# Attention pooling with a gated feed-forward layer on one core: the same instructions in another written-out order

## The chip, the cores and the metric

The kernel runs on one core of one Trainium2 chip. The metric is the device time of one execution in microseconds. The core has five engines, each with an instruction stream of its own that it works through in order: TensorE (PE, matmuls; its weight loads are listed as PEld), VectorE (DVE), ScalarE (ACT), GpSimd (POOL) and SyncE (SP). In this kernel the input loads are issued by POOL and the stores, and the copies inside the chip, by SP.

## The reference

Four batches of x (12480 rows of 128) meet 32 inducing rows I twice, and the result goes through one feed-forward layer:

```python
def mab(q, kv):
    s = scale * (q @ kv.transpose(0, 2, 1))
    s = s - s.max(-1, keepdims=True)
    a = np.exp(s)
    a /= a.sum(-1, keepdims=True) + 1e-09
    return a @ kv
h = mab(I, x)          # 32 rows for each batch: pooling over all of x
y = mab(x, h)          # every row of x attends to those 32 rows
u = y @ w_in           # 128 -> 2048
out = (u * np.clip(u + 3.0, 0.0, 6.0) / 6.0) @ w_out
```

## The kernel before, in words

Each batch is cut into six groups of 2048 rows and a short one (group 6) of 192 rows. For every batch there are two passes over the groups. The first is the pooling; it needs all groups of the batch before its result is there. Then a few small steps turn the 32 pooled rows into tables of the feed-forward layer. The second pass makes the output of every group out of its transposed rows, which are kept on the chip from the first.

The whole order of the work is one text, `ORDER` (lines 23 to 165): a list of tokens, each a call of a function `op_...` with its arguments: the batch, the group, a range or a part, the PSUM bank (0 to 7), and a letter for the engine where more than one can do it (V for DVE, A for ACT, P for POOL). The loop at lines 816 to 818 emits them one after the other, so the text fixes the order on every engine's queue. Tiles stand in small rings of buffers, and an instruction waits for those that it depends on.

First pass, for batch b and group g:
- `X` (line 416) loads rows of x into one of five xr buffers, issued on POOL's queue. A buffer is free when the casts and the last `A` of the group five before have read it.
- `K` (line 420) casts to bf16 on one of three engines, `T` (line 426) transposes 8 blocks of 128 rows on PE, `Y` (line 432) copies them out of PSUM.
- `S` (line 437) makes the scores with I on PE, `E` (line 445) the exponential on ACT, `A` (line 453) the weighted sums on PE, `H` (lines 464 and 466) adds them up on DVE, `D` (lines 471 and 473) adds up the weights.

Between the passes, for a batch: `c1` to `c9`, `cA` and `cB` (lines 477 to 526) with `c3` (lines 492 and 493), the sum of the weights over the partitions by two matmuls with ones; `G`, `L` and `cH` to `cN` (lines 545 to 589); 16 `M` (line 532, PE) with 16 `N` (line 540, Square on ACT); 16 `P` (line 598, PE) and `cP` (line 608).

Second pass, for a group:
- `Z` (line 621, PE) with `Zd` (line 631) and `Ze` (line 636), two exponentials on ACT. `Zd` writes one of two dk buffers.
- `W` (line 642): four copies by DMA from SP's queue, which spread dk over the partitions into one of two d buffers.
- `R` (line 650, PE), `Rl` (line 655, Ln on ACT), `Rz` (line 660, DVE), `Ra` (line 674, Exp on ACT), `Rh` (line 685, DVE).
- `B` (line 693, PE), `F` (line 703, Exp on ACT), `U` (line 712, DVE, which reads d), for the two halves of a group.
- `l` (line 729), `q` (line 747), both PE, add up the output in a bank; `v` (line 758) copies it out on DVE or ACT, and `O` (line 767) stores a group from SP's queue.

Four more tokens matter here. `it` (line 334) asks ACT for one activation table that has both Exp and Ln. ACT needs the right table for its functions, and where the order gives it another function than the table at hand has, the build puts a table load ahead of the instruction. `i1` (masks.py) makes the identity matrix on POOL, `i6` and `i7` constants there. `w.n.k` (line 353) is n matmuls of 512 columns over a tile of zeros into bank k, whose result nobody reads:

```python
def op_it(e):
    nc.scalar.preload_act_table_set("natural_log_exp_and_others")

def op_w(n, k):
    for _ in range(n):
        nc.tensor.matmul(ps[:, k, :], lhsT=wake[:, :P], rhs=wake)
```

The weights are loaded once (`wi`, `wo`, lines 393 and 396) and split or cast by `wh`, `wl` and `wb` (lines 403 to 409). At the end a few checks on ranges (`y0` to `yb`) give one flag; only if it is set does a slow path run (line 824).

Of the kernel before, what the change touches and what calls it, by code (L numbers as in the profile page):

```python
# [28 lines left out]
E.0.1.0.16.5 Y.0.2.8.16.3.A A.0.1.0.8.5 S.0.2.0.8.7 T.0.3.8.16.4 K.0.3.0.8.V S.0.2.8.16.7 D.0.1.V i6.P Y.0.3.8.16.4.V
i7.P A.0.1.8.16.5 E.0.2.0.16.7 T.0.3.0.8.2 H.0.0.1 wh.0.V H.0.1.5 wh.1.A A.0.2.0.8.7 Y.0.3.0.8.2.A wh.3.A wh.2.A  # L30
X.0.5.0.16 wl.1.V A.0.2.8.16.7 D.0.2.V K.0.4.0.8.V X.1.0.0.16 wo.- wl.2.V S.0.3.0.8.2 S.0.3.8.16.2 H.0.2.7 T.0.4.0.8.6
E.0.3.0.16.2 A.0.3.0.8.2 Y.0.4.0.8.6.A X.1.1.0.16 K.0.4.8.16.P K.0.5.8.16.P T.0.4.8.16.1 A.0.3.8.16.2 X.1.2.0.16
S.0.4.0.8.4 K.0.5.0.8.A D.0.3.V Y.0.4.8.16.1.V S.0.4.8.16.4 E.0.4.0.16.4 K.1.0.0.8.P T.0.5.0.8.5 wl.3.V T.0.5.8.16.1
Y.0.5.8.16.1.A Y.0.5.0.8.5.V A.0.4.0.8.3 S.0.5.0.8.5 A.0.4.8.16.3 S.0.5.8.16.5 H.0.3.2 E.0.5.0.16.5 K.1.0.8.16.V H.0.4.3
T.1.0.8.16.1 Y.1.0.8.16.1.A wb.1.A A.0.5.0.8.4 wb.0.A A.0.5.8.16.4 D.0.4.V D.0.5.V c1.0.- X.1.3.0.16 T.1.0.0.8.3 H.0.5.4
H.0.6.0 X.1.4.0.16 Y.1.0.0.8.3.A c3.0.6 K.1.1.0.8.P c5.0.7 c4.0.6 S.1.0.0.8.3 S.1.0.8.16.3 c6.0.7 c9.0.V wb.2.A
Z.0.1.2.7 c7.0.A Z.0.0.5.6 c8.0.V K.1.1.8.16.V wb.3.A G.0.1.4 E.1.0.0.16.3 Zd.0.1.2 T.1.1.0.8.3 T.1.1.8.16.0 cA.0.V
cB.0.V Ze.0.0.6 M.0.0.2 R.0.0.1 Zd.0.0.5 wl.0.V M.0.7.5 Ze.0.1.7 G.0.2.4 G.0.0.4 Y.1.1.8.16.0.V G.0.3.4 Rl.0.0.1
N.0.0.2.A Y.1.1.0.8.3.V M.0.2.1 M.0.3.0 M.0.6.2 K.1.2.8.16.P Rz.0.0.6 R.0.1.3 N.0.7.5.A M.0.1.6 N.0.2.1.A Rl.0.1.3
Rh.0.0.V cH.0.4 S.1.1.0.8.5 A.1.0.0.8.1 Rz.0.1.7 N.0.6.2.A S.1.1.8.16.5 M.0.8.3 A.1.0.8.16.1 M.0.10.7 M.0.5.2 N.0.3.0.A  # L40
W.0.0 P.0.2.0 K.1.2.0.8.P P.0.3.0 K.1.3.0.8.V H.1.0.1 E.1.1.0.16.5 T.1.2.8.16.1 M.0.9.5 D.1.0.V Rh.0.1.V N.0.1.6.A
N.0.10.7.A cJ.0.4 N.0.8.3.A T.1.2.0.8.7 T.1.3.0.8.3 M.0.4.6 Y.1.2.8.16.1.V M.0.11.1 K.1.3.8.16.P cI.0.4 P.0.1.0
X.1.5.0.16 Y.1.3.0.8.3.V N.0.9.5.A M.0.14.5 M.0.13.4 X.1.6.0.2 Ra.0.1 D.1.1.V K.1.4.8.16.P N.0.5.2.A Y.1.2.0.8.7.V
P.0.0.0 A.1.1.0.8.2 M.0.12.3 P.0.7.0 N.0.11.1.A N.0.13.4.A P.0.5.0 P.0.11.0 S.1.2.0.8.7 K.1.4.0.8.V P.0.9.0 A.1.1.8.16.2
Ra.0.0 H.1.1.2 N.0.4.6.A S.1.2.8.16.7 N.0.14.5.A N.0.12.3.A L.0.0.6 B.0.0.0.2.4 X.2.0.0.16 E.1.2.0.16.7 P.0.4.0
T.1.3.8.16.7 K.1.5.0.8.V L.0.1.6 F.0.0.0.1.4 P.0.14.0 Y.1.3.8.16.7.V W.0.1 Z.0.2.1.4 K.1.5.8.16.V Z.0.3.7.5 K.1.6.0.2.A
cL.0.6 F.0.0.0.0.2 M.0.15.3 P.0.12.0 P.0.6.0 Zd.0.3.7 Zd.0.2.1 cM.0.2 P.0.10.0 U.0.0.0 P.0.8.0 cN.0.2 N.0.15.3.A
T.1.6.0.2.1 Ze.0.2.4 P.0.13.0 P.0.15.0 B.0.0.1.2.6 Y.1.6.0.2.1.A T.1.5.0.8.1 cP.0.0 Y.1.5.0.8.1.V q.0.0.0.0.0
q.0.0.0.1.0 Ze.0.3.5 T.1.4.0.8.1 F.0.0.1.0.2 R.0.2.2 F.0.0.1.1.6 D.1.2.P Rl.0.2.2 U.0.0.1 Rz.0.2.4 K.2.0.0.8.V l.0.0.1.3
l.0.0.0.0 l.0.0.2.6 l.0.0.3.7 q.0.0.1.0.3 v.0.0.0.0.A Rh.0.2.V q.0.0.1.1.3 S.1.3.0.8.0 T.1.4.8.16.2 Y.1.4.0.8.1.A  # L50
v.0.0.1.3.A S.1.3.8.16.0 q.0.0.2.0.6 E.1.3.0.16.0 Y.1.4.8.16.2.V W.0.2 q.0.0.2.1.6 B.0.1.0.0.2 q.0.0.3.0.7 D.1.3.P
A.1.2.0.8.4 q.0.0.3.1.7 Ra.0.2 A.1.2.8.16.4 F.0.1.0.0.0 K.2.0.8.16.V v.0.0.2.6.V A.1.3.0.8.6 F.0.1.0.1.2 H.1.2.4 U.0.1.0
v.0.0.3.7.A B.0.2.0.0.2 T.1.5.8.16.7 F.0.2.0.1.2 F.0.2.0.0.0 A.1.3.8.16.6 l.0.1.0.4 Y.1.5.8.16.7.V q.0.1.0.0.4
q.0.1.1.0.7 B.0.2.1.2.0 H.1.3.6 S.1.4.0.8.6 q.0.1.0.1.4 v.0.1.0.4.V S.1.4.8.16.6 q.0.1.1.1.7 F.0.2.1.1.0 l.0.1.1.7
F.0.2.1.0.2 R.0.3.1 O.0.0.0.16 l.0.2.1.4 X.2.1.0.16 v.0.1.1.7.V E.1.4.0.16.6 l.0.2.0.0 U.0.2.0 Rl.0.3.1 q.0.2.1.0.4
B.0.1.1.6.2 Rz.0.3.5 A.1.4.0.8.1 q.0.2.0.0.0 F.0.1.1.1.2 F.0.1.1.0.6 D.1.4.V q.0.2.0.1.0 U.0.1.1 q.0.2.1.1.4 S.1.5.0.8.2
A.1.4.8.16.1 X.2.2.0.16 q.0.1.2.0.5 v.0.2.1.4.A S.1.5.8.16.2 q.0.1.3.0.7 Rh.0.3.V K.2.1.8.16.P Z.0.4.4.6 v.0.2.0.0.A
H.1.4.1 E.1.5.0.16.2 B.0.3.0.2.0 W.0.3 D.1.5.V Zd.0.4.4 q.0.1.2.1.5 q.0.1.3.1.7 A.1.5.0.8.4 K.2.1.0.8.P F.0.3.0.0.2
# [10 lines left out]
D.2.0.P q.0.4.0.0.3 M.1.0.5 l.0.4.0.3 Rh.0.6.V v.0.4.1.4.V F.0.4.1.0.6 F.0.4.1.1.0 N.1.0.5.A O.0.3.0.16 U.0.4.1
B.0.5.0.6.0 q.0.4.2.0.4 q.0.4.0.1.3 M.1.1.5 L.1.1.2 F.0.5.0.0.6 v.0.4.0.3.V cL.1.2 F.0.5.0.1.0 q.0.4.2.1.4 B.0.5.1.6.0  # L70
W.0.6 U.0.5.0 q.0.4.3.0.2 M.1.4.3 N.1.1.5.A F.0.5.1.1.0 l.0.4.2.4 N.1.4.3.A l.0.4.3.2 v.0.4.2.4.V M.1.8.5 F.0.5.1.0.6
q.0.5.0.0.0 q.0.4.3.1.2 N.1.8.5.A Z.1.0.3.1 Z.1.1.6.4 v.0.4.3.2.V Ra.0.6 Zd.1.0.3 S.2.1.0.8.2 M.1.10.5 l.0.5.0.0
q.0.5.0.1.0 S.2.1.8.16.2 M.1.5.3 Ze.1.0.1 P.1.2.7 Zd.1.1.6 U.0.5.1 v.0.5.0.0.V cM.1.6 R.1.0.0 O.0.4.0.16 P.1.3.7
# [906 lines left out]
```

## Time and profile before

| what | value |
|---|---|
| median of three runs | 308.41 us (304.93 to 309.09) |
| the profiled execution, its time | 310.61 us |
| its span, first to last instruction | 308.8 us |
| busy: PE, ACT, DVE, POOL | 275.8, 255.7, 218.5, 65.7 us |
| moved by DMA | 66.69 MB, mean 216 GB/s |
| shares of the chain that ended last | PE 64%, ACT 13%, DVE 9%, DMA 7%, issue 3% |

The busy time of PE counts each matmul from start to its modelled end, so overlapping ones hide how much room is left; how fast PE goes when nothing holds it is read from the chain of waits, where each piece is the time by which it moved the end. Prices of one instruction on the other engines are read from the groups by line.

### The profile page before, as it was taken

The numbers are of one execution on the slowest core, as the hardware profiler recorded it, in microseconds if no ns is written. First come the engines' busy times: TensorE is split into PE (matmuls) and PEld (weight loads), VectorE is DVE, ScalarE is ACT, GpSimd is POOL, SyncE is SP. The second block draws the span as 40 slices with busy tenths as digits, with TensorE's granted clock in tenths as the row PEclk, the third lists the DMA queues.
The fourth block names the chain that finished last, engine by engine and source line by source line (L and its number), as shares of the span: only waits on it lengthen the run. The fifth ranks groups of instructions, "written<-read, shape, count | busy, mean of one in ns | idle before, by whom it ended". The sixth has DMA issues, their size and how long they took to land.

```text
span 308.8 us, 9738 instructions
## 1 busy us (share of the span) xinstructions
PE 275.8 (89%) x4105; PEld 216.8 (70%) x4105; DVE 218.5 (71%) x386; ACT 255.7 (83%) x416; POOL 65.7 (21%) x101
## 2 busy tenths in 40 slices
...
GB/s 154 419 348 409 346 248 153 138 70 330 212 326 293 2 142 179 184 231 182 338 385 240 138 183 42 197 156 240 180 104 270 248 141 69 222 231 244 326 163 155
DMA packets 23312, 66.69 MB, mean 216 GB/s; under 512 B 3648, under 2 KB 16736, under 8 KB 16992
## 3 DMA queue, kind: packets, MB, share of 16 engines
...
q8 instruction: 33, 0.54, 0.7%
q14 instruction: 15, 0.12, 0.1%
...
## 4 chain that ended last, share of the span: by engine, by line
PE 64%; ACT 13%; DVE 9%; DMA 7%; issue 3%; SPq 1%; POOL 0%; ACTq 0%; DVEq 0%; POOLq 0%
PE ps L747 25%; PE ps L729 7%; PE ps L426 6%; PE ps L453 5%; DMA d<-dk 5%; PE ps L693 5%; PE ps L598 4%; PE ps L532 3%; ACT TF L703 3%; PE ps L621 3%; DMA xl<-in_x_dram 2%; PE ps L437 2%; ACT L655 2%; PE ps L650 2%; DVE TD L712 2%
## 5 line engine op out<-in xcount | busy, mean ns | idle before, releaser
L703 ACT ACTIVATE TF<-ps 128x1024 bf16<-128x1024 f32 (+1 forms) x100 | 96.2, 1005 | 8.8 <-PE ps L693 7.3
L712 DVE TENSOR_TENSOR TD<-TF,d 128x2048 bf16<-128x2048 bf16 (+1 forms) x52 | 61.1, 1177 | 13.3 <-ACT TF L703 11.7
L747 PE MATMUL ps<-Cq,TD 128*128 128x128 bf16 (+1 forms) x784 | 59.9, 222 | 0.1
L747 PE MATMUL ps<-Cq,TF 128*128 128x128 bf16 (+1 forms) x784 | 59.3, 221 | 0.2
L758 DVE COPY os<-ps 128x512 f32<-128x512 f32 x62 | 42.2, 688 | 22.8 <-PE ps L747 17.8
L747 PEld LDWEIGHTS <-TF 128*128 128x128 bf16 (+1 forms) x784 | 46.6, 99 | 11.2 <-issue 9.1
L747 PEld LDWEIGHTS <-TD 128*128 128x128 bf16 (+1 forms) x784 | 47.4, 100 | 6.9 <-issue 4.6
L729 PE MATMUL ps<-BD,a 128*128 128x512 f32 (+1 forms) x100 | 39.2, 463 | 0.0
L420 POOL CAST xb<-xr 128x1024 bf16<-128x1024 f32 x24 | 28.1, 1180 | 51.7 <-PE ps L426 39.1
L540 ACT ACTIVATE sq<-ps 128x512 bf16<-128x512 f32 x64 | 35.2, 617 | 1.5 <-PE ps L532 1.4
L453 PE MATMUL ps<-xr,a 128*32 128x128 f32 x384 | 31.8, 229 | 3.1 <-ACT ln L655 2.2
L426 PE MATMUL ps<-ident_b,xb 128*128 128x128 bf16 x384 | 30.8, 232 | 3.0 <-DVE xb L420 1.8
L432 DVE COPY xT<-ps 128x1024 bf16<-128x1024 bf16 x32 | 21.8, 687 | 13.0 <-PE ps L426 11.9
L453 PEld LDWEIGHTS ps<-xr,a 128*32 128x32 f32 x384 | 25.4, 111 | 5.6 <-ACT ln L655 3.0
L426 PEld LDWEIGHTS <-xb 128*128 128x128 bf16 x384 | 24.9, 105 | 6.1 <-issue 3.7
L693 PE MATMUL ps<-z,pair 32*128 32x256 f16 (+1 forms) x400 | 21.3, 272 | 7.9 <-ACT os L758 2.4
L416 POOL DMA_DIRECT2D xr<-in_x_dram x25 | 15.7, 630 | 49.5 <-PE ps L453 26.2
L532 PE MATMUL ps<-dH,w_hi 128*128 128x512 bf16 x64 | 22.2, 384 | 3.3 <-ACT dk L631 1.8
L758 ACT COPY os<-ps 128x512 f32<-128x512 f32 x34 | 19.7, 590 | 4.9 <-PE ps L747 2.7
L660 DVE CUSTOM_DVE_ANT_0 zz<-ln,ps 128x512 f32<-128x512 f32 (+1 forms) x28 | 17.3, 619 | 9.0 <-ACT ln L655 8.8
L729 PEld LDWEIGHTS ps<-BD,a 128*128 128x128 f32 (+1 forms) x100 | 18.3, 196 | 4.9 <-ACT dk L631 2.0
L432 ACT COPY xT<-ps 128x1024 bf16<-128x1024 bf16 x16 | 16.2, 1015 | 5.1 <-PE ps L426 5.1
...
## 6 DMA issues: line engine op xcount, KB each, us to landing
...
```

Of the source, the lines that this page charges most:

```text
L420: copier(e)(at(xb, xbl, b, g)[:p, lo:hi, :], at(xr, xl, b, g)[:p, lo:hi, :].bitcast(FP32))
L426: nc.tensor.transpose(pt[:, (i - lo) * p : (i - lo + 1) * p], at(xb, xbl, b, g)[:p, i, :], ident_b[:p, :p])
L432: copier(e)(xT_of(b, g)[:, lo * p : hi * p], ps[:, k, :].bitcast(BF16)[:, : (hi - lo) * p])
L453: nc.tensor.matmul(ps[:M, k, :C], lhsT=at(a1, a1l, b, g)[:p, i * M : (i + 1) * M], rhs=at(xr, xl, b, g)[:p, i, :], start=(i == 0), stop=(i ...
L532: nc.tensor.matmul(ps[:, k, :], lhsT=w_hi[:, jb, :], rhs=dH[:, :, :, :, :].rearrange("p q k m i -> p (q k m i)"),)
L540: nc.scalar.activation(sq_of(b, jb)[:, :], ps[:, k, :], ACT.Square)
L693: nc.tensor.matmul(ps[:, pairs[j // 2] + j % 2, f * w : (f + 1) * w], lhsT=pair[rows, f].rearrange("p m i -> p (m i)"), rhs=fat(z_, b, g)[ ...
L703: nc.scalar.activation(hat(TF_, b, g, h)[:, 2 * q : 2 * q + 2, :w], ps[:, k : k + 2, :w], ACT.Exp, scale=-1.0)
L712: nc.vector.tensor_mul(split(hat(TD_, b, g, h)), split(hat(TF_, b, g, h)), d.unsqueeze(2).to_broadcast([P, J, 2, w]),)
L729: nc.tensor.matmul(ps[:p, k, : J * C], lhsT=fat(a_, b, g)[:rows, s * p : (s + 1) * p], rhs=BD_[b % 2][:rows, :J, :].rearrange("p j c -> p ...
L747: nc.tensor.matmul(ps[:p, k, j * C : (j + 1) * C], lhsT=t[:, j, f * w + s2 * p : f * w + (s2 + 1) * p], rhs=Cq_[b % 2][:, (1 + f) if u els ...
L758: copier(e)(at(os_, osl, b, g)[:p, s * J : (s + 1) * J, :], ps[:p, k, : J * C].rearrange("p (j c) -> p j c", c=C),)
```

## The change

Only the text of `ORDER` is replaced: 1599 tokens in place of 1583, where the 16 more are all `w` (24 with 48 matmuls in place of 8 with 16, all of them in the pooling of batch 0). Every other operation is there as often as before. What differs is the place of each, the bank, and for some the engine:

| operation | before | after |
|---|---|---|
| K, cast of x | 26 P, 22 V, 4 A | 24 P, 17 V, 11 A |
| Y, copy of the transposed rows | 33 V, 19 A | 41 V, 11 A |
| v, copy of the output | 65 V, 35 A | 61 V, 39 A |
| D, sum of the weights | 15 V, 9 P | 12 V, 12 P |
| wh, wb, parts of the weights | 1 V 3 A, 4 A | 2 V 2 A, 2 A 2 P |

`it` is the first token; before, it stood in the middle of batch 1's tables. The first five loads of x stand ahead of everything else on POOL's queue, and the short group 6 of batch 0, which was first through PE, comes among the full ones. The diff, cut to the start and to the places that the text below speaks of:

```diff
-i0.- X.0.0.8.16 i1.- X.0.0.0.8 i2.- w.2.6 X.0.6.0.2 w.2.0 i4.5 K.0.6.0.2.A w.2.3 w.2.0 w.2.2 i3.V T.0.6.0.2.4 i8.- w.2.3
-w.2.7 i5.5.V X.0.1.0.16 i9.P X.0.2.0.16 ia.- K.0.0.8.16.V Y.0.6.0.2.4.A X.0.3.0.16 S.0.6.0.2.0 E.0.6.0.2.0 w.2.2
...
-v.0.2.3.2.V q.0.2.2.0.3 O.0.1.0.16 q.0.2.2.1.3 B.0.3.1.0.4 X.2.4.0.16 Y.2.0.0.8.7.A W.0.4 c3.1.7 K.2.2.0.8.P
...
-T.2.1.8.16.1 cA.1.V M.1.2.0 Zd.0.6.4 Ze.0.6.5 Rz.0.4.6 l.0.3.0.4 R.0.5.6 c9.1.P E.2.0.0.16.2 Y.2.1.8.16.1.A T.2.1.0.8.2
...
-N.1.10.5.A E.2.1.0.16.2 q.0.5.1.0.5 N.1.5.3.A Rl.1.0.0 M.1.11.3 M.1.7.2 D.2.1.P it.- N.1.7.2.A A.2.0.0.8.0 cN.1.6
...
+it.- i2.- X.0.0.0.8 w.2.2 X.0.0.8.16 X.0.1.0.16 w.2.5 X.0.2.0.16 w.2.3 w.2.1 X.0.3.0.16 i1.- w.2.2 i9.P w.2.6 w.2.7
+w.2.3 i0.- i3.V w.2.5 i4.3 w.2.7 K.0.0.0.8.A w.2.4 i8.- K.0.0.8.16.A w.2.6 T.0.0.0.8.2 X.0.6.0.2 ia.- T.0.0.8.16.0
+i5.3.V w.2.3 w.2.1 Y.0.0.8.16.0.A i6.P Y.0.0.0.8.2.V w.2.2 K.0.1.0.8.V K.0.1.8.16.A S.0.0.0.8.7 S.0.0.8.16.7 T.0.1.0.8.2
+X.0.4.0.16 T.0.1.8.16.5 E.0.0.0.16.7 A.0.0.0.8.1 D.0.0.V w.2.0 Y.0.1.0.8.2.A Y.0.1.8.16.5.V K.0.2.8.16.A S.0.1.0.8.4
+A.0.0.8.16.1 w.2.0 S.0.1.8.16.4 K.0.2.0.8.V T.0.2.0.8.5 T.0.2.8.16.2 E.0.1.0.16.4 A.0.1.0.8.4 wi.- Y.0.2.0.8.5.V w.2.0
+Y.0.2.8.16.2.A H.0.0.1 X.0.5.0.16 K.0.3.0.8.A K.0.6.0.2.P A.0.1.8.16.4 S.0.2.0.8.1 T.0.6.0.2.6 D.0.1.V S.0.2.8.16.1
...
+R.1.0.5 E.2.1.0.16.0 l.0.5.0.0 Rl.1.0.5 W.0.6 X.2.5.0.16 l.0.5.3.2 q.0.5.3.1.2 Y.2.2.0.8.1.V P.1.6.6 Rh.0.6.V
...
+T.2.3.0.8.7 K.2.4.8.16.P v.0.5.0.0.V P.1.15.6 K.2.6.0.2.V F.0.6.0.0.2 Zd.1.1.5 Ra.1.0 K.2.5.0.8.V q.0.5.1.0.4
...
+X.3.5.0.16 cM.2.4 F.1.5.1.1.6 X.3.6.0.2 K.3.6.0.2.A Y.3.2.8.16.3.V cN.2.4 l.1.5.1.6 l.1.5.0.3 K.3.4.8.16.P E.3.1.0.16.0
...
```

More of the change, by code (lines that the diff above doesn't have):

```diff
@@ L29 @@
[L29 to L58, printed above, removed]
@@ L69 @@
[L69 to L73, printed above, removed]
@@ new lines @@
+wh.0.A D.0.3.V H.0.3.7 Y.0.4.8.16.6.A wh.3.A K.0.5.0.8.A X.1.1.0.16 wo.- S.0.4.0.8.2 wl.0.V K.0.5.8.16.V w.2.7
+S.0.4.8.16.2 w.2.3 T.0.5.8.16.6 wh.2.V E.0.4.0.16.2 T.0.5.0.8.1 wl.3.V A.0.4.0.8.2 A.0.4.8.16.2 Y.0.5.0.8.1.V
+Y.0.5.8.16.6.A K.1.0.0.8.V S.0.5.0.8.1 S.0.5.8.16.1 T.1.0.0.8.7 X.1.2.0.16 K.1.0.8.16.A D.0.4.V T.1.0.8.16.3
+E.0.5.0.16.1 X.1.3.0.16 A.0.5.0.8.6 H.0.4.2 D.0.5.V w.2.2 c1.0.- A.0.5.8.16.6 Y.1.0.0.8.7.A Y.1.0.8.16.3.A K.1.1.8.16.A
+S.1.0.0.8.5 H.0.5.6 K.1.1.0.8.P c3.0.7 S.1.0.8.16.5 H.0.6.4 T.1.1.0.8.4 wl.2.V E.1.0.0.16.5 c5.0.0 c4.0.7 c6.0.0
@@ new lines @@
+q.0.0.3.0.3 q.0.0.3.1.3 X.2.2.0.16 H.1.3.1 K.2.0.8.16.V F.0.1.0.1.6 B.0.1.1.0.6 Ra.0.2 Y.1.6.0.2.5.V q.0.0.2.0.2
+v.0.0.3.3.A U.0.1.0 q.0.0.2.1.2 S.1.4.0.8.3 q.0.1.0.0.4 T.1.5.0.8.5 S.1.4.8.16.3 Rh.0.3.V F.0.1.1.0.0 v.0.0.2.2.V
+Y.1.5.0.8.5.V T.1.5.8.16.2 q.0.1.0.1.4 O.0.0.0.16 S.1.5.0.8.5 Y.1.5.8.16.2.V F.0.1.1.1.6 S.1.6.0.2.0 E.1.4.0.16.3
+q.0.1.1.0.1 B.0.2.0.6.2 E.1.6.0.2.0 K.2.0.0.8.P S.1.5.8.16.5 D.1.4.P A.1.4.0.8.0 v.0.1.0.4.V c2.1.- q.0.1.2.0.4
+A.1.4.8.16.0 U.0.1.1 F.0.2.0.1.2 q.0.1.1.1.1 W.0.3 F.0.2.0.0.6 K.2.1.8.16.V B.0.2.1.2.6 E.1.5.0.16.5 q.0.1.2.1.4 H.1.4.0
@@ new lines @@
+F.0.2.1.1.6 A.1.5.0.8.5 l.0.2.0.0 l.0.1.1.1 l.0.1.3.6 F.0.2.1.0.2 l.0.1.2.4 X.2.3.0.16 A.1.6.0.2.7 U.0.2.0 D.1.5.P
+v.0.1.2.4.V A.1.5.8.16.5 X.2.4.0.16 H.1.5.5 q.0.1.3.0.6 q.0.1.3.1.6 Ra.0.3 v.0.1.1.1.A v.0.1.3.6.V B.0.3.0.2.4
+q.0.2.0.0.0 q.0.2.0.1.0 q.0.2.1.0.6 H.1.6.7 O.0.1.0.16 c5.1.1 l.0.2.1.6 F.0.3.0.1.4 c1.1.- l.0.2.3.7 q.0.2.1.1.6
+F.0.3.0.0.2 v.0.2.0.0.A B.0.3.1.2.4 c3.1.0 v.0.2.1.6.A U.0.2.1 q.0.2.3.0.7 c4.1.0 c6.1.1 F.0.3.1.1.4 c7.1.A q.0.2.2.0.6
+cB.1.V q.0.2.3.1.7 c8.1.V v.0.2.3.7.V Z.0.4.4.5 Z.0.5.1.0 T.2.0.0.8.7 F.0.3.1.0.2 Ze.0.4.5 cA.1.V M.1.0.2 Zd.0.4.4
```

219 lines of the change are left out of this document (118 added, 101 removed).

## The prediction, made before the result was known

> **What bounds the kernel now.** I read the page's span and the chain of waits first, then busy time by stage, then the groups by line, then the landing times. I cut the span at op c3 (line 492), which sums the softmax weights of a batch over the partitions and so closes its pooling; it comes once for each of the four batches.
>
> ```profile
> span 308.8 us, 9738 instructions
> ```
> ```profile
> 34.56 0.41 PE ps L492 x2
> ...
> 45.04 1.28 ACT L445
> 46.34 0.60 ACT a L445
> ...
> 86.73 8.02 DMA d<-dk
> ...
> 121.57 1.28 ACT L655
> ...
> 153.53 7.16 DMA d<-dk
> ...
> 230.11 0.34 PE ps L492 x2
> ```
> ```profile
> 88.13 0.41 PE L492 MATMUL ps<-dred,ones 128*128 128x32 f32 x2
> 158.85 0.41 PE L492 MATMUL ps<-dred,ones 128*128 128x32 f32 x2
> ```
> The columns of the chain are start, length and who held it. The next fence gives each stage between those marks: length, then busy time of PE, PEld, DVE, ACT and POOL, then the granted clock.
> ```profile
> 0.00:34.56 34.56, 26.25 (x328) 20.23 (x328) 23.32 (x44) 18.30 (x25) 15.35 (x42) 0.85 0.93 333
> 34.56:88.13 53.57, 46.89 (x749) 37.35 (x749) 38.60 (x69) 50.13 (x81) 16.48 (x18) 1.00 0.65 214
> 88.13:158.85 70.72, 62.44 (x933) 49.43 (x929) 47.10 (x81) 61.41 (x97) 19.69 (x24) 0.95 0.65 214
> 158.85:230.11 71.26, 68.43 (x1052) 54.44 (x1048) 54.13 (x93) 58.99 (x101) 12.60 (x14) 0.98 0.54 173
> 230.11:302.44 72.33, 71.76 (x1053) 55.38 (x1053) 55.40 (x103) 66.86 (x116) 1.59 (x4) 1.00 0.64 211
> 302.44:308.80 6.36, 0.00 (x0) 0.00 (x0) 0.00 (x1) 0.00 (x0) 0.00 (x0) 0.78 0.43 158
> ```
> Stages four and five are PE's: 68.43 of 71.26 and 71.76 of 72.33. Stage two is ACT's (50.13 of 53.57), and stage three is nobody's: ACT is busy 61.41 of 70.72, PE 62.44, and two waits for the copy d<-dk of 8.02 and 7.16 us stand in the chain around there. What ACT does besides its work is in the groups by line:
> ```profile
> L655 ACT ACT_TABLE_LOAD x7 | 9.0, 1283 | 2.0 <-PE ps L650 1.9
> L445 ACT ACT_TABLE_LOAD x2 | 2.6, 1283 | 0.0
> L674 ACT ACT_TABLE_LOAD x2 | 2.6, 1283 | 0.0
> L420 ACT ACT_TABLE_LOAD x1 | 1.3, 1283 | 0.7 <-PEq L964 0.7
> L703 ACT ACT_TABLE_LOAD x1 | 1.3, 1283 | 0.0
> L636 ACT ACT_TABLE_LOAD x1 | 1.3, 1283 | 0.0
> L334 ACT ACT_TABLE_LOAD x1 | 1.3, 1283 | 0.0
> ```
> That is 15 loads of 1.283 us. They come in pairs, one before a Ln (L655) and one before the next Exp (L445, L674, L703, L636). The request on line 334 stands at the end of them; after it 20 more Ln stand in the order among the Exps, and no load follows. By their starts, one lies in stage one, six in stage two (7.7 us) and eight in stage three (10.3 us, the one at line 334 among them). From 45.04 to 121.57 eight are links of the chain itself, 10.3 us.
>
> **The change part by part.** *The table request first.* One load remains, at the start, where ACT waits for data anyway: its 1.28 us cost nothing, and would cost 1.28 us if the first data were there at once. The other 14, 18.0 us of ACT, go. What this is worth is bounded by 10.3 us (those in the chain) and 18.0 us; it needs PE to be able to follow, which is the sum below. The chain gives the price of one load: the next ACT instruction starts at 46.34, 0.02 us after the load's end. The Trainium skill (ScalarE: Activation LUTs, What ACT_TABLE_LOAD costs) says that a switch of sets costs the 1283 ns and a drain of about 1380 ns besides; the load agrees with the rows, the drain does not show in them. By that rule the eight links would be worth another 11 us, and my sum would be 276 instead of 287.
>
> *The work that PE has in each stage.* Every operation is still there, so only its place moves. I price PE by what the chain shows for its kinds when nothing holds it:
> ```profile
> 139.22 0.39 PE ps L437 x16
> ...
> 187.16 0.33 PE ps L693 x8
> ...
> 188.49 0.22 PE ps L532
> 188.71 0.23 PE ps L729
> 188.93 0.91 PE ps L598 x16
> ...
> 194.07 0.46 PE ps L747 x8
> ...
> 194.73 0.98 PE ps L621 x16
> ...
> 196.00 0.90 PE ps L426 x16
> ...
> 198.43 0.48 PE ps L453 x8
> ...
> 242.86 0.29 PE ps L549 x12
> ```
> So one q op is 0.46, T 0.45, A 0.48, S 0.20, Z 0.49, B 0.33, l 0.23, M 0.22, P 0.23 (four matmuls), G 0.29; R is priced as l and L as A, being of the same shape. Counted in the two orders (an op of the short last group as a quarter), stages two to five hold, before then after: q 24 then 20, 40.5 and 40.5, 50.5 and 53.5, 79 and 80; l 12 then 11, 20.25 and 18.25, 24.25 and 27.25, 40.5 and 40.5; Z 5 then 4, 7.25 and 6.25, 5.25 and 8.25, 7.5 and 6.5; B 8 and 8, 9.25 and 8.25, 14.25 and 14.25, 17.5 and 18.5; R 4 and 4, 6.25 and 5.25, 7.25 and 8.25, 7.5 and 7.5; T 11.25 then 10.25, 11.25 and 12.25, 12.25 and 12.25, none; S 12.25 then 11.25, and 12.25 twice; A 12.25 three times; 16 M, 16 P, 4 G and 2 L each. In PE time: 42.5 then 39.3; 54.0 and 53.0; 60.9 and 64.7; 66.2 and 66.5.
>
> How much of a stage such a price fills when PE sets the pace is read from stage five: 66.2 of 72.33, or 0.915 (the rest is small matmuls that I have not priced, and their fill). Stage four before is 60.9 of 71.26, with a stall in it:
> ```profile
> 160.87 1.08 ACT L631 ACTIVATE dk<-ps 128x512 bf16<-128x512 f32 x2 [2.67 <-DMA d<-dk]
> ```
> Without these 2.67 us and the 1.4 us that its mean clock of 0.98 stands for, it is 60.9 of 67.2, 0.91. Stages two and three reach 0.79 and 0.76 only.
>
> *After, stage by stage.* Five: 66.5/0.915 = 72.7. Four: 64.7/0.915 = 70.7. Three: 53.0/0.915 = 57.9, plus 3 us of waits (below) = 61. There ACT's own work of before is 61.41 - 10.3 = 51.1, so it fits. Two: 39.3/0.915 = 43.0, plus 3 us for the row from c3 to the first M, where PE has only a few transposes and scores of the next batch to do = 46; ACT's work there is 50.13 - 7.7 = 42.4 at most. The moves of copies between engines change little: ACT takes over 7 K and 4 v and gives up 8 Y, 1 wh and 2 wb; DVE the reverse; POOL takes over 3 D and 2 wb and gives up 2 K. Each is about one to seven us over the whole span on engines that PE now outlasts.
>
> *Stage one.* It holds the same work, with loads in another order and 48 idle matmuls instead of 16.
> ```profile
> 10.08 1.71 PE ps L353 x4
> ```
> ```profile
> 11.70 0.69 DVE L420 CAST xb<-xr 128x1024 bf16<-128x1024 f32 x1 [1.95 <-DMA xr<-in_x_dram]
> ...
> 25.14 1.47 POOL L420 CAST xb<-xr 128x1024 bf16<-128x1024 f32 x1 [0.59 <-DVE dacc L473]
> ```
> ```profile
> 10.00:20.00 10.00, 9.80 (x124) 7.92 (x123) 5.63 (x11) 5.61 (x8) 0.29 (x1) 0.71 1.06 417
> ```
> The input comes at 417 GB/s, and by 11.70 us groups 0 and 1 are in (2.2 MB with the short group). In the new queue of POOL the first five loads come one after the other, then the short one, group 4, the first weight and group 5, which is released by the last A of group 0. I take that release at about 15 us, before the queue runs dry. Up to the end of group 5 there are 7.4 MB; 11.5 + 5.3 MB at 417 GB/s = 24.3 us. Before, the last cast of group 5's first half started at 25.14 and c3 at 34.56, 9.4 us later with DVE busy all that time. Its pure row of cast, transpose, copy, score, exp, sum and reduction is about 5 us. I take 6.7 between these: c3 at 31, with 29 and 34 as ends. The idle matmuls: 24 stand before the first transpose, at 0.43 us each (1.71 for four) 10.3 us, so it starts by 11.8 at the latest, or at about 9 if the clock rises on the way; before, the first full group's transposes started behind 12.76 us. The other 24 cost 5.3 us at M's 0.22. PE's price here is 14.9/0.915 + 5.3 = 21.6 us: from 9 us on that ends at 31 too, from 11.8 at 33.4. They are free only while data is late; that cover gone, stage one ends at the upper bound.
>
> *The waits that move.* Zd (line 631) may write one of two dk buffers only when the four copies W of two groups before have landed, and ACT stands behind it with everything in its queue.
> ```profile
> DMA to landing us min/median/max: 1.8/3.2/8.3
> ```
> ```profile
> DMA to landing us min/median/max: 4.6/7.3/15.4
> ```
> These are the landings of d, then of xr. In PE's price, the way from W's release (its Zd, the U that frees d, the stores ahead of it on SP) to that Zd is under 8 us for 10 of 26 groups before, and the two that stood in the chain have 7.3 and 6.7. After, it is under 8 for 4: 6.2 (group 6 of batch 0), 5.7, 6.3 and 6.4. So I expect one such wait, not two: the 3 us in stage three. The end stays 6.36 us: the last store and what follows it.
>
> *Sum:* 31 + 46 + 61 + 70.7 + 72.7 + 6.4 = 287.8 us of span, 21.0 under 308.8. The profiled execution took 310.61 us, 1.8 beside its span; 287.8 + 1.8 = 289.6. The runs shown have their median at 308.41, 2.2 below that execution, so **287 us**.
>
> **The rivals.** *A, PE never starved:* stage one ends at 29 and neither 3 us is lost: 8 us less, 279. For it: the wider gaps; against it: before, even without loads, DVE and PE handed the row behind c3 to and fro. *B, the order is no better than the old one apart from the loads:* only the eight links go, 308.4 - 10.3 = 298. For it: stage three lost more to waits than to loads, and new waits can stand where these stood. *C, the loads come back,* since the request stands before other requests: with 14 loads stages two and three are ACT's again (42.4 + 7.7 = 50 and 51.1 + 10.3, over 0.87 as before, 70.6); 4 + 9.6 us more, 300. Against it: nothing was loaded behind line 334. *D, slower: the x loads come too late for the casts that DVE and ACT now stand on.* For X.2.0, X.2.1, X.2.5 and X.3.6 the cast comes 7.3, 8.9, 6.9 and 7.3 us of PE's price after the load can go out; at the median landing of 7.3 us that costs next to nothing, at 15.4 it costs 8.1 + 6.5 + 8.5 + 8.1 = 31 us: 318. It decides from a landing of about 12.6 us on, where the four waits eat up the 21 us. Against it: these are bursts of one or two loads, and only stage one's queue is long. *E, a load holds ACT longer than its row,* by as much again: eight times 1.28 us more, 277; the 0.02 us behind the load speak against it.
>
> **How the numbers follow.** Forecast 0.53, A 0.18, B 0.17, C 0.04, D 0.06, E 0.02. The range 275 to 302 goes at the low end past A and E by two to four us, for c3 of batch 0 can't well come before 29 but stages two and three may each lose less than I take, and at the high end past B and C by as much; D is left out. A measurement of this kernel can tell about 2%, 6.2 us, from no change. Slower by more than that is most of D, 0.05; within it are the rest of D and the upper ends of B and C, 0.09; faster is 0.86.
>
> **What would show it.** Right: one table load in the groups by line; c3 near 31, 77, 138 and 209 us; ACT no longer above PE in stage two; at most one d<-dk wait of several us in the chain; stages four and five as long as now within 2 us. Wrong: 14 loads still there (C); casts on DVE or ACT that wait for xr by more than 5 us in all in the list of waits (D); stage three still near 70 us with d<-dk in the chain (B); stage one past 34 us with PE busy on line 353, which would mean that the idle matmuls have no cover.

## The result and the profile after

The changed kernel takes 285.69 us (median of 4 runs, 285.12 to 286.46) against 308.75 us for the one before (304.93 to 309.3): a ratio of 0.928, with an interval of 0.920 to 0.936. The forecast was 287 us in a range of 275 to 302. The profiled execution of after took 285.83 us, 1.7 us beside its span. Before has faster and slower executions, the slower ones at a lower mean clock of PE: gains in the experiments are read against its faster ones in the same series (medians 306.5 us beside e1, e2, e3 and e6, 306.0 beside e7 and e9, 305.5 beside e10 to e12), while its profiled execution (310.61 us, clock 0.962) and that of e9c (0.955) are slow ones, so that before's stages are 2 to 5 us too long in all and e9c is not read by stage. Against those medians the gain of after is 19 to 21 us, against the four runs above 23; the prediction's sum was for 21 us of span.

The page of after: the span, and busy time with its share of the span.

```profile
span 284.1 us, 9800 instructions
...
PE 271.7 (96%) x4125; PEld 211.4 (74%) x4137; DVE 212.1 (75%) x387; ACT 238.5 (84%) x402; POOL 64.8 (23%) x100
```

PE was busy 271.7 us, 275.8 before, so most of the gain (20.6 of 24.7 us of span) is time in which PE had stood still: 308.8 - 275.8 = 33 us before, 12.4 now, and half of that is the end, where only the last store is under way. ACT lost 17.2 us, close to 14 loads of 1.28. The groups by line have one load left:

```profile
L335 ACT ACT_TABLE_LOAD x1 | 1.3, 1283 | 0.7 <-PEq L965 0.7
```

The timeline of PE has c3, the cut between the stages, at these times (the first and the last of four):

```profile
30.68 0.41 PE L493 MATMUL ps<-dred,ones 128*128 128x32 f32 x2
...
202.78 0.35 PE L493 MATMUL ps<-dred,ones 128*128 128x32 f32 x2
```

Busy time between these cuts, in the columns of the prediction's table: length, busy time (and instructions) of PE, PEld, DVE, ACT and POOL, the granted clock, the busy share of the DMA engines, GB/s.

```profile
0.00:30.68 30.68, 28.95 (x364) 20.38 (x368) 19.59 (x41) 21.48 (x27) 13.61 (x41) 1.00 0.97 367
30.68:74.07 43.39, 42.63 (x698) 34.41 (x695) 37.81 (x69) 38.58 (x68) 17.80 (x21) 1.00 0.77 259
74.07:133.01 58.94, 57.19 (x919) 46.34 (x917) 45.58 (x79) 49.84 (x89) 16.44 (x19) 1.00 0.74 253
133.01:202.78 69.77, 69.56 (x1096) 54.72 (x1099) 52.16 (x91) 61.60 (x108) 17.00 (x19) 1.00 0.61 193
202.78:277.70 74.92, 73.35 (x1063) 55.54 (x1062) 56.93 (x109) 67.00 (x115) 0.00 (x0) 1.00 0.61 200
277.70:284.10 6.40, 0.00 (x0) 0.00 (x0) 0.00 (x0) 0.00 (x0) 0.00 (x0) 0.63 0.36 128
```

Stage two fell by 10.2 us, stage three by 11.8, stage one by 3.9, stage four by 1.5; stage five grew by 2.6. (Before's clock was 0.85 in stage one and 0.95 in stage three; what this is worth is told at the end of the account below.) ACT is no longer above PE in stage two, 38.58 us against 42.63. PE is now busy for 97 to 99.7% of each of stages two to five. The chain of waits (start, length, who) shows how the first transposes follow the idle matmuls of line 354, and that four waits for d<-dk, 29 us in all, stand in it:

```profile
1.19 6.55 PE ps L354 x18
7.91 1.40 PE ps L354 x6
9.31 0.89 PE ps L427 x16
...
67.52 10.80 DMA d<-dk
...
102.43 6.13 DMA d<-dk
...
122.58 6.92 DMA d<-dk
...
136.44 5.22 DMA d<-dk
```

Whether these 29 us cost anything is a question for an experiment, for PE is busy in all of the 10.80 us of the longest. Two windows that lie over most of it, and the list of waits (total, times, longest), where the engines that need these copies stand idle for them by 3.3 us in all:

```profile
64.00:70.00 6.00, 6.00 (x98) 5.09 (x96) 4.74 (x7) 5.25 (x9) 2.04 (x3) 1.00 0.99 354
70.00:76.00 6.00, 6.00 (x97) 4.85 (x97) 4.61 (x11) 4.92 (x8) 1.62 (x2) 1.00 1.03 352
```
```profile
DVE TD L713 <- DMA d<-dk: 2.5, 2, 1.3
ACT dk L632 <- DMA d<-dk: 0.8, 2, 0.4
```

So two of the four links stand ahead of U, which reads d (67.52 and 122.58), and two ahead of Zd, which needs a free dk buffer (102.43 and 136.44).

### The profile page after: what moved, and what is told of

It reads as the page before. It is cut to its first block, busy times and chain, and to the rows that moved or that the text cites. A ratio compares the mean times of both kernels' runs of the same rounds, so it can differ in the third digit from the quotient of the medians.

```text
span 284.1 us, 9800 instructions
## 1 busy us (share of the span) xinstructions
PE 271.7 (96%) x4125; PEld 211.4 (74%) x4137; DVE 212.1 (75%) x387; ACT 238.5 (84%) x402; POOL 64.8 (23%) x100
## 4 chain that ended last, share of the span: by engine, by line
PE 72%; DMA 10%; DVE 8%; issue 3%; ACT 3%; SPq 2%; ACTq 0%; DVEq 0%
PE ps L748 25%; DMA d<-dk 10%; PE ps L730 7%; PE ps L599 5%; PE ps L427 5%; PE ps L454 5%; PE ps L694 5%; PE ps L533 4%; PE ps L354 4%; PE ps L622 4%; DVE TD L713 3%; PE ps L438 2%; PE ps L651 2%; SPq L643 2%; PE ps L550 2%
## 5 line engine op out<-in xcount | busy, mean ns | idle before, releaser
L748 PE MATMUL ps<-Cq,TD 128*128 128x128 bf16 (+1 forms) x784 | 58.6, 220 | 0.0
L759 DVE COPY os<-ps 128x512 f32<-128x512 f32 x60 | 40.8, 687 | 19.2 <-PE ps L748 17.0
L748 PEld LDWEIGHTS <-TF 128*128 128x128 bf16 (+1 forms) x784 | 45.7, 98 | 9.9 <-issue 9.1
L421 POOL CAST xb<-xr 128x1024 bf16<-128x1024 f32 x23 | 24.8, 1087 | 60.9 <-PE ps L427 49.7
L433 DVE COPY xT<-ps 128x1024 bf16<-128x1024 bf16 x38 | 25.5, 685 | 7.4 <-PE ps L427 6.0
L427 PE MATMUL ps<-ident_b,xb 128*128 128x128 bf16 x384 | 27.8, 219 | 1.0 <-DVE os L759 0.5
L759 ACT COPY os<-ps 128x512 f32<-128x512 f32 x36 | 21.0, 592 | 6.8 <-PE ps L748 6.6
L427 PEld LDWEIGHTS <-xb 128*128 128x128 bf16 x384 | 22.4, 98 | 5.1 <-issue 3.1
L417 POOL DMA_DIRECT2D xr<-in_x_dram x25 | 14.5, 585 | 50.0 <-PE ps L454 26.3
L533 PE MATMUL ps<-dH,w_hi 128*128 128x512 bf16 x56 | 20.5, 381 | 0.2
L599 PE MATMUL ps<-w_ob,sq 128*128 128x128 bf16 x256 | 20.7, 220 | 0.0
L730 PEld LDWEIGHTS ps<-BD,a 128*128 128x128 f32 (+1 forms) x100 | 17.2, 189 | 3.1 <-issue 0.5
```

The costliest lines, as they stand in the source:

```text
L427: nc.tensor.transpose(pt[:, (i - lo) * p : (i - lo + 1) * p], at(xb, xbl, b, g)[:p, i, :], ident_b[:p, :p])
L433: copier(e)(xT_of(b, g)[:, lo * p : hi * p], ps[:, k, :].bitcast(BF16)[:, : (hi - lo) * p])
L533: nc.tensor.matmul(ps[:, k, :], lhsT=w_hi[:, jb, :], rhs=dH[:, :, :, :, :].rearrange("p q k m i -> p (q k m i)"),)
L599: nc.tensor.matmul(ps[:, k, f * C : (f + 1) * C], lhsT=sq_of(b, jc)[:, f * P : (f + 1) * P], rhs=w_ob[:, jc, :], start=(sums_of[b] == 1 an ...
L730: nc.tensor.matmul(ps[:p, k, : J * C], lhsT=fat(a_, b, g)[:rows, s * p : (s + 1) * p], rhs=BD_[b % 2][:rows, :J, :].rearrange("p j c -> p ...
L748: nc.tensor.matmul(ps[:p, k, j * C : (j + 1) * C], lhsT=t[:, j, f * w + s2 * p : f * w + (s2 + 1) * p], rhs=Cq_[b % 2][:, (1 + f) if u els ...
```

## The experiments

The theory: the one request takes 14 loads off ACT; with that PE sets the pace in stages two to five, so that the time is PE's work at about nine tenths; stage one is set by its input. The rivals: that the order rather than the request brings the gain, that links of the chain (d<-dk) still cost time, that the idle matmuls matter, and that the loads of x in a row do not.

### e1: only the request moved, in the order of before

```diff
-i0.- X.0.0.8.16 i1.- X.0.0.0.8 ...
+it.- i0.- X.0.0.8.16 i1.- X.0.0.0.8 ...
...
-M.1.7.2 D.2.1.P it.- N.1.7.2.A
+M.1.7.2 D.2.1.P N.1.7.2.A
```

> The order of before with only the table request moved to its start. Both theories expect one table load left instead of 15. Theory (the loads that were links of the chain are worth their length, the other ones little): 308.7 less 10.3 us, 298 us, and not under 291, which is all 18.0 us. Rival 1 (the loads were hidden, the whole gain is the order's): 306 to 309 us. Rival 2 (the loads are the whole gain and the order gives nothing): 286 us.

Measured: 294.23 us (292.06 to 295.93), a ratio of 0.955 (0.943 to 0.967); beside 306.5 it gains 12.3 us. The theory's 298 us, from the eight loads in the chain alone, is missed by 4 us but its bound of 291 holds, and both rivals (306 to 309 and 286) fall. The groups by line of e1 have the one load, and its windows between the c3s read:

```profile
L337 ACT ACT_TABLE_LOAD x1 | 1.3, 1283 | 0.7 <-PEq L967 0.7
```
```profile
33.76:82.73 48.97, 46.00 (x749) 37.23 (x749) 38.23 (x68) 42.52 (x75) 17.21 (x18) 1.00 0.72 230
82.73:144.88 62.15, 59.95 (x933) 47.88 (x930) 45.90 (x81) 51.42 (x89) 18.80 (x24) 0.97 0.74 247
144.88:214.28 69.40, 67.18 (x1051) 53.03 (x1048) 54.53 (x93) 58.86 (x101) 13.51 (x14) 1.00 0.56 179
214.28:286.90 72.62, 71.83 (x1057) 55.44 (x1053) 55.47 (x103) 66.68 (x116) 1.59 (x4) 1.00 0.64 211
```

Stage two is 4.6 us shorter than before with six loads (7.7 us) gone, stage three 8.6 with eight (10.3 us) gone. Each of the 14 loads was worth 12.3/14 = 0.88 us, less than its own 1.28, which fits loads that lay in part beside other waits; that was not looked at load by load. Stages four and five hold no load and change by -1.9 and +0.3.

### e2: the new order with the request late

```diff
-it.- i2.- X.0.0.0.8 w.2.2 ...
+i2.- X.0.0.0.8 w.2.2 ...
...
-Y.2.1.8.16.2.V N.1.13.5.A A.2.0.0.8.3
+Y.2.1.8.16.2.V N.1.13.5.A it.- A.2.0.0.8.3
```

> The order of after with only the table request moved back to where it stood before, ahead of the first pooling sum of batch 2. Theory (ACT has room beside PE in the new order only without the loads): 14 or so loads come back in stages two and three; ACT's work there grows to 46 and 60 us against lengths of 43.4 and 58.9, so stages two and three get longer by 10 to 14 us and the time is 296 to 300 us. Rival (PE bounds these stages in the new order and hides the loads): under 290 us.

Measured: 302.02 us (300.95 to 302.71), a ratio of 0.981 (0.971 to 0.991) to before: 16.3 us more than after. The theory's 296 to 300 is missed by 2 us: its reason held, but the two stages grew by 16.0 us and not by 10 to 14. ACT's timeline has 14 loads, 13 more than after; behind the one at the start these are the first and the last, and the windows of stages two and three follow.

```profile
37.82 1.28 ACT L659 ACT_TABLE_LOAD   x1
...
115.67 1.28 ACT L338 ACT_TABLE_LOAD   x1
```
```profile
31.84:84.38 52.54, 44.90 (x693) 34.74 (x693) 37.03 (x69) 48.66 (x75) 17.48 (x21) 1.00 0.64 215
84.38:150.15 65.77, 59.66 (x921) 47.64 (x917) 45.55 (x79) 56.37 (x94) 16.21 (x19) 0.97 0.65 219
```

Eight loads (10.3 us) lengthen stage two by 9.2 us, five (6.4 us) stage three by 6.8. In this order a load shows at 16.3/13 = 1.25 us, almost all of it. So with the request the order is worth 294.23 - 285.69 = 8.5 us, without it 306.5 - 302.02 = 4.5; the request is worth 12.3 in the old order and 16.3 in the new. (Beside e12, a later series of after, 8.5 and 16.3 become 7.6 and 15.4.) Neither the request nor the order is the whole gain: each brings a part.

The Trainium skill (ScalarE: Activation LUTs, What ACT_TABLE_LOAD costs) adds a drain of 1380 ns to each switch of sets. An estimate by it is 34.6 us for the 13 loads; 16.3 were measured, which the load's own 1.283 us accounts for.

### e3: no idle matmuls

Every `w` token is taken out, 24 with 48 matmuls.

```diff
-X.0.0.0.8 w.2.2 X.0.0.8.16 X.0.1.0.16 w.2.5 X.0.2.0.16 w.2.3 w.2.1 X.0.3.0.16 ...
+X.0.0.0.8 X.0.0.8.16 X.0.1.0.16 X.0.2.0.16 X.0.3.0.16 ...
```

> The order of after without any of the 48 idle matmuls, which give nothing to the output. Theory of the prediction (they only fill time in which the data is late, and the clock's state changes the first transposes only): stage one ends within 2 us of 30.7 us and the time is 284 to 288 us. Rival 1 (they keep the clock up through the pooling of batch 0): the granted clock falls to half for several us in stage one, c3 comes 3 us or more later, 289 us or more. Rival 2 (they stand in PE's way): c3 comes earlier, 282 us or less.

Measured: 287.35 us (286.01 to 290.64), a ratio of 0.932 (0.919 to 0.944), not to be told apart from after (285.12 to 286.46, and 284.15 to 286.92 in e12). PE's timeline in stage one:

```profile
6.78 1.04 PE L428 MATMUL ps<-ident_b,xb 128*128 128x128 bf16 x8 [1.76 <-ACT xb L422]
...
10.74 1.87 PE L428 MATMUL ps<-ident_b,xb 128*128 128x128 bf16 x16
...
30.27 0.41 PE L494 MATMUL ps<-dred,ones 128*128 128x32 f32 x2 [0.45 <-DVE dred L479]
```

Without the idle matmuls the first transposes start at 6.78 instead of 9.31 us but run at half speed (1.87 us for 16 at 10.74 us, where after needs 0.89), and c3 comes at 30.27 beside 30.68. The start gained and the speed lost cancel before the input is in. Stage three of e3 is 61.12 us long, 2.2 more than after's, though no idle matmul stood there: a single stage of one execution can differ by that much without an edit in it.

### e6: a third dk buffer

```diff
-        dk_ = ring("dk", 2, [P, 512], BF16)
+        dk_ = ring("dk", 3, [P, 512], BF16)
...
-        junk = sb.tile([P, B * M], FP32, name="junk")
+        junk = r6
```

The second edit makes the room for the buffer.

> The order of after with three dk buffers instead of two (the scratch tile of the checks at the end shares memory with another one to make room), so that the exponential into dk waits for the copies of three groups before. Theory (PE is busy 57.2 of the 58.9 us of stage three, so the d<-dk links of the chain stand beside PE's work and cost at most those 1.7 us and little elsewhere): 284 to 286 us. Rival (the d<-dk links, 29 us of the chain in the profile after, set the end; a fair part of them goes): 282 us or less.

Measured: 284.64 us (284.37 to 284.94), a ratio of 0.925 (0.916 to 0.933). The chain of e6 still has d<-dk, twice, both times ahead of U, and stage three is as long as after's 58.94:

```profile
67.56 11.09 DMA d<-dk
...
123.40 5.64 DMA d<-dk
```
```profile
73.62:132.59 58.97, 57.00 (x922) 46.19 (x918) 45.05 (x79) 49.91 (x89) 15.13 (x19) 1.00 0.72 249
```

The two links ahead of Zd (6.13 and 5.22 us) left the chain and the time fell by about 1 us, 2 beside e12, at the edge of what can be measured. A third buffer for d as well, which might remove the two ahead of U, was not tried.

### e9a, e9b, e9c: more work for PE

`x.n.k` is n matmuls of 512 columns over a weight tile into bank k, whose result is overwritten by the Z that follows. Two of them stand ahead of each Z of a full group: of batches 2 and 3 in e9a, of batches 0 and 1 in e9b, and of batches 0 and 1 in the order of before in e9c.

```diff
+def op_x(n, k):
+    for _ in range(n):
+        nc.tensor.matmul(ps[:, k, :], lhsT=w_hi[:, 0, :], rhs=w_hi[:, 0:4, :].rearrange("p a c -> p (a c)"))
...
-Z.2.0.5.1
+x.2.5 Z.2.0.5.1
```

> The order of after with two more matmuls of 512 columns ahead of each Z of the full groups of batches 2 and 3, 24 Z in all, half of them in stage four and half in stage five; each writes a bank that Z overwrites next, so the output is the same. 48 matmuls of 0.216 us, 10.4 us of PE. Theory (PE sets the pace in stages four and five): all of it shows, 5.2 us in each stage, 295 to 297 us. Rival (ACT, which is busy 61.6 of 69.8 and 67.0 of 74.9 us, sets the pace there with PE only looking busy): stages four and five take up at least half of it, 291 us or less.

> The same in the order of after for batches 0 and 1: 48 matmuls, 16 of them in stage two, 24 in stage three, 8 in stage four, 10.4 us of PE. Theory (since the loads are gone, PE sets the pace in stages two and three as well): 294 to 297 us, stage two 3.5 and stage three 5.2 us longer. Rival (waits of the chain for the copies d<-dk and for DVE set stage three, and PE has room beside them): 290 us or less.

> The same in the order of before for batches 0 and 1, its table loads kept: 48 matmuls, 20 of them in stage two and 28 in stage three, 10.4 us of PE. Theory (before, ACT with its loads set the pace there, so that PE had room): 4 us or less on top of before, 312 us or less. Rival (PE set the pace before as well, and the loads' gain came through something else): 316 us or more.

Where these expectations count 48 matmuls or 10.4 us they miscount: twelve Z with two each make 24, at 0.216 us 5.2 us (in e9a 12 in stage four and 12 in stage five, 2.6 us each); six idle matmuls of the same width take 1.29 us in after's chain, 0.215 each. With the count halved the theories' times become about 290 to 291.5 us for e9a and e9b, and the rivals' 288 or less. Measured:

| kernel | median (range), us | ratio to before | more than without them, of 5.2 us |
|---|---|---|---|
| e9a | 292.09 (291.18 to 292.36) | 0.951 (0.945 to 0.958) | span +5.3, median +5.5 (e12) to +6.4 |
| e9b | 289.28 (288.88 to 290.05) | 0.942 (0.935 to 0.949) | span +3.4, median +2.7 (e12) to +3.6 |
| e9c | 309.23 (306.75 to 315.0) | 1.007 (1.002 to 1.013) | by the ratio 2.2 (0.6 to 3.9) |

The windows of e9a, stages four and five, then of e9b, stages two and three:

```profile
132.88:205.32 72.44, 71.56 (x1103) 55.32 (x1111) 52.26 (x91) 62.49 (x109) 16.99 (x19) 1.00 0.58 190
205.32:283.00 77.68, 75.52 (x1071) 56.34 (x1074) 56.99 (x109) 66.92 (x114) 0.00 (x0) 1.00 0.58 190
```
```profile
30.13:75.66 45.53, 44.62 (x703) 34.65 (x703) 37.62 (x69) 39.24 (x68) 16.99 (x21) 1.00 0.73 248
75.66:136.06 60.40, 58.96 (x927) 46.67 (x930) 45.18 (x79) 50.07 (x89) 16.29 (x19) 1.00 0.72 249
```

Stages four and five grew by 2.67 and 2.76 us for 2.6 each: there PE sets the pace outright. Stage two grew by 2.1 for 1.7 (8 matmuls), stage three by 1.5 for 2.6 (12), together 3.6 for 4.3: there it does mostly, as far as one execution tells when a stage can differ by 2 us. The time of e9b lies between its theory and its rival. In the order of before less than half of such work shows. The last is the weakest of the three, since its interval reaches from a tenth to three quarters.

### e7 and e10: the old queue of first loads in the new order

In e7 POOL's first loads and constants stand as before, with the weight wi ahead of group 4. e10 is e7 with the halves of group 0 the other way round, as after has them.

```diff
-it.- i2.- X.0.0.0.8 w.2.2 X.0.0.8.16 X.0.1.0.16 w.2.5 X.0.2.0.16 w.2.3 w.2.1 X.0.3.0.16 i1.- w.2.2 i9.P ...
+it.- X.0.0.8.16 i1.- X.0.0.0.8 i2.- X.0.6.0.2 X.0.1.0.16 i9.P X.0.2.0.16 X.0.3.0.16 wi.- X.0.4.0.16 w.2.2 ...
```

> The order of after with the first entries of POOL's queue in the order of before: the second half of group 0 first, the identity matrix, the first half, the short group, group 1, the small constants, groups 2 and 3, the first weight, group 4. Theory (stage one is paced by the input, and its end by group 5, behind which the same bytes stand in both orders): the first transposes are late by 3 us but c3 by 2 us at most, 285 to 288 us. Rival (loads back to back are what makes stage one shorter): c3 at 33.5 us or later, 289 us or more.

> As the run with the old order of POOL's queue, but with the first half of group 0, which the new order casts first, loaded first. Theory A (there, c3 was 3.3 us late because the half that the order wants first came second): c3 at 31.5 us or earlier, 286 to 287 us. Theory B (it is late because the small work between the loads and the short group hold the first full groups back, which moves the release of group 5's buffer): c3 at 32.5 us or later, 288 us or more.

Measured: e7 290.15 us (288.19 to 291.28), a ratio of 0.943 (0.935 to 0.950), so 3.5 to 4.5 us more than after by its two series; e10 288.93 us (287.22 to 291.15), 0.946 (0.938 to 0.954), 2.3 more than after in its series. With c3 at 33.97 us e7 bears out its rival: the theory had c3 later by 2 us at most, and it is 3.3. Timelines, first of after (casts of group 0, then of groups 4 and 5), then of e7 and of e10; the bracket is the wait ahead of the instruction.

```profile
5.66 1.04 ACT L421 CAST xb<-xr 128x1024 bf16<-128x1024 f32 x1 [3.63 <-DMA xr<-in_x_dram]
...
19.16 1.04 POOL L421 CAST xb<-xr 128x1024 bf16<-128x1024 f32 x1
...
24.73 0.67 DVE L421 CAST xb<-xr 128x1024 bf16<-128x1024 f32 x1
```
```profile
9.55 1.99 ACT L424 CAST xb<-xr 128x1024 bf16<-128x1024 f32 x2 [7.53 <-DMA xr<-in_x_dram]
...
22.38 1.04 POOL L424 CAST xb<-xr 128x1024 bf16<-128x1024 f32 x1 [1.28 <-DMA xr<-in_x_dram]
...
33.97 0.41 PE L496 MATMUL ps<-dred,ones 128*128 128x32 f32 x2 [0.60 <-DVE dred L481]
```
```profile
5.63 1.04 ACT L424 CAST xb<-xr 128x1024 bf16<-128x1024 f32 x1 [3.61 <-DMA xr<-in_x_dram]
...
22.90 1.04 POOL L424 CAST xb<-xr 128x1024 bf16<-128x1024 f32 x1 [2.88 <-DMA xr<-in_x_dram]
23.99 1.04 PE L430 MATMUL ps<-ident_b,xb 128*128 128x128 bf16 x8 [2.00 <-POOL xb L424]
...
29.24 0.67 DVE L424 CAST xb<-xr 128x1024 bf16<-128x1024 f32 x1
...
36.08 0.41 PE L496 MATMUL ps<-dred,ones 128*128 128x32 f32 x2 [0.78 <-DVE dred L481]
```

Which half comes first decides when ACT starts (9.55 or 5.63 us). How much of e7's loss that is stays open: two of e10's four runs took 287.2 and 287.3 us, within a microsecond of after's 286.63, and two 290.6 and 291.2. The profiled one is the slowest of them; its c3 comes at 36.08, and in it PE stands still for 2.00 us and then, from 24 us on, runs at a granted clock of 0.50 for 3.4 us. What the profiles of e7 and e10 share is group 4, cast 3.2 and 3.7 us later and with a wait for its load that after does not have. Group 5's load goes out at 17.10 and 16.02 us, at 15.09 in after, and its DVE cast starts at 27.32 and 29.24. The first ten microseconds, after and then e7:

```profile
0.00:10.00 10.00, 8.81 (x41) 3.87 (x42) 3.56 (x12) 3.37 (x3) 7.26 (x30) 1.00 0.75 265
```
```profile
0.00:10.00 10.00, 8.58 (x25) 3.07 (x25) 2.34 (x11) 1.73 (x2) 7.32 (x30) 1.00 0.69 207
```

The same queue moves 265 GB/s with five loads in a row and 207 with constants between them, 0.6 MB less in ten microseconds. How much of the 3 us of stage one is this and how much the weight ahead of group 4 was not taken apart.

### e11 and e12: weights later, and after once more

In e11 the third dk buffer of e6 stands, and four preparations of weights move: the casts `wh.0.A` and `wh.3.A` to the end of stage one, behind its last exponential, and the subtractions `wl.0.V` and `wl.3.V` into stage two. e12 is after, unchanged, in the same series.

```diff
-wh.0.A D.0.3.V H.0.3.7 Y.0.4.8.16.6.A wh.3.A K.0.5.0.8.A
+D.0.3.V H.0.3.7 Y.0.4.8.16.6.A K.0.5.0.8.A
...
-T.1.0.8.16.3 E.0.5.0.16.1 X.1.3.0.16
+T.1.0.8.16.3 E.0.5.0.16.1 wh.0.A wh.3.A X.1.3.0.16
```

> The order of after with three dk buffers, and with two of the weight casts (on ACT) and the two subtractions behind them (on DVE), which waited for the weight's load on the way to the last groups of batch 0, put behind the last exponential of batch 0 and behind the tables for the feed-forward layer. Theory (in the last 9 us of stage one the chain goes over these two casts and the casts of group 5 on ACT; taking them out brings c3 forward by up to 2 us): c3 at 28.5 to 30 us, 282.5 to 284.5 us. Rival (the work only comes back in stage two, where PE waits for the same tables): 284.5 to 286 us.

> The kernel after once more, beside the run with three dk buffers and later weight casts on the same chip. All theories: 284.5 to 286.5 us.

Measured: e11 288.21 us (286.86 to 292.27), a ratio of 0.946 (0.941 to 0.951); e12 286.63 us (284.15 to 286.92), 0.939 (0.934 to 0.943), a tenth above its range. e11 misses theory and rival: it is slower than both, and c3 comes at 31.44 us, not at 28.5 to 30. Its chain ahead of c3:

```profile
28.27 0.76 ACT w_hi L407
...
29.15 1.11 ACT w_hi L407
30.25 1.83 ACT xT L436 x2
```

The two preparations now stand between the last exponential and the copies of batch 1 and hold these up; stage two is 45.7 us instead of 43.4, and stage three 57.1 instead of 58.9. No version here beats after by more than e6's 1 to 2 us.

## Why the prediction was right, and where its steps were off

- **Stage one, c3 at 31.** Right: 30.68. The release of group 5's load was taken at 15 us and its arrival priced at 24.3; the load goes out at 15.09 and its DVE cast starts at 24.73. That the idle matmuls are free while data is late holds (e3). That the order of POOL's queue sets this stage is shown by e7: c3 3.3 us later with the old queue, at a granted clock of 1.00 in both.
- **The table loads, between 10.3 and 18.0 us.** Right: 12.3 in the old order (e1). The price of one load, its own 1.28 us and nothing besides, is shown by e2 (1.25 each): in the new order almost all of a load shows.
- **PE's price at 0.915 of a stage.** The step holds: 39.3, 53.0, 64.7 and 66.5 us of priced work over the measured stages give 0.906, 0.899, 0.927 and 0.888. e9a shows the ground of it in stages four and five, every added microsecond of PE appearing in the time; for stages two and three e9b shows it in part.
- **The two allowances of 3 us.** These terms were mis-sized. Stage two was to lose 3 us on the row behind c3; it measured 43.4 in place of 46, 0.4 above the bare 43.0. Stage three was to lose 3 us to a wait of Zd for d<-dk; it measured 58.9 in place of 61, 1.0 above 57.9. In it ACT stands 0.4 us at most ahead of such a Zd, and e6, without that wait, has a stage three of 58.97.
- **"At most one d<-dk wait of several us in the chain".** Wrong: there are four. The step behind it, a wait in the chain as a loss, failed. The chain follows what came last for each instruction, and a copy of 10.80 us is such a link although PE is busy 6.00 of 6.00 us on both sides of 70 us, and the two links ahead of Zd, 11.4 us long, were worth 1 to 2 us (e6).
- **Stage five, 72.7 us.** Off by 2.2: 74.9. "As long as now within 2 us" is missed by 0.6 (72.33 before). The loss is partly at the end, where PE is busy 11.43 of the last 12.70 us:

```profile
265.00:277.70 12.70, 11.43 (x168) 9.51 (x165) 8.68 (x20) 8.24 (x15) 0.00 (x0) 1.00 0.65 237
```

  PE also needs 73.35 us of busy time where 71.76 had done (73.3 to 73.7 in every profile of the new order that adds nothing there, 71.8 in e1); why was not tested.
- **The sum.** 287.8 us of span against 284.1: -0.3, -2.6, -2.1, -0.9 and +2.2 for the five stages. The forecast of the time was better than its terms, and this by luck: stage five made up for part of the two allowances.
- **The rivals.** B (only the loads count) falls: the order adds 8.5 us. A (279 us) had the two allowances right, but not a stage one of 29 us, and stage five was longer than it took. C falls with the one load in the profile. D falls: ACT's casts wait 4.1 us for xr, all of it for the two loads of group 0, and DVE's not at all (it waits 1.0 us for a short group's load), under the 5 us that were to show it. (Its four ways add up to 30.4 us, so that 21 us more are reached at a landing of 12.9 us, not 12.6.) E falls with e2, where a load costs no more than its row.

What the order does in stages two to four is seen between e1 and after, where the loads are gone from both. Stage four takes 3.8 us more of priced PE work and is 0.4 us longer, as it had gaps in e1 (PE 67.18 of 69.40) and has none now (69.56 of 69.77). Stages two and three give up 4.2 us of that work and are 8.8 us shorter. How much of the rest is the better interleaving of copies and how much the banks was not separated.

Something else may stand behind these differences, the granted clock. In windows of 0.1 us it falls to 0.50 behind several waits of PE of 1.5 to 3.9 us, for 3.4 or 6.8 us each time: four times in before, 20.5 us in all (from 9, 26, 101 and 163 us on), twice in e1 (from 25 and 86 us), once in e2 (from 99 us). One of before's is in this window, behind a wait of 2.40 us for ACT:

```profile
100.00:120.00 20.00, 16.74 (x206) 12.23 (x205) 11.72 (x21) 17.87 (x30) 0.00 (x0) 0.83 0.19 72
```

In after PE waits for 1.2 us at most and the clock stays at 1.00 until its last matmul. So closing the gaps may pay twice. An estimate from these lengths is that up to 10 us of PE's time were lost in before, 3.4 in e1, that is up to 3.4 of the 8.5 us of the order, and none in after. No run separates this part, and where PE did not set the pace it costs less.
